# One eighth of a group's output weights as 64-partition rows over the first eight DMA engines

## The chip, the cores and the metric

The kernel runs on one core of one Trainium2 chip. The metric is device time in microseconds (us) of a whole execution. Single executions of one kernel agree within about 0.1% (the six of the kernel before, 382.23 to 382.36), so differences of a few tenths of a microsecond out of 382 need several runs on each side and, better, a look at the trace. Where two times are compared as a ratio, it is the mean time of one kernel's runs over the mean of the other's runs of the same rounds, so it is not quite the ratio of the medians that are quoted.

## The reference, cut to what matters

One token passes through an attention block with a cached K and V and through a gated MLP; a scalar gate mixes the two.

```python
q = (x @ wq)                       # 32 heads of 128
scores = q @ k_cache * Dh ** -0.5  # 4 kv heads, 65536 cached positions
o = softmax(scores) @ v_cache      # 32 x 128 = 4096 numbers
a = o.reshape(1, 1, 4096) @ wo     # wo: 4096 x 1024, bf16, 8 MiB
...
return g * a + (1 - g) * b         # b: the gated MLP
```

K and V caches are 64 MiB each. Almost all the work is to move 162 MB from device memory into SBUF, the on-chip memory.

## The kernel before

A fixed list of large loads is issued by one queue, each as soon as its place in a ring of SBUF is free. The last loads are the four groups of `wo`, the output weights. A group is 1024 rows; partition p holds rows 8p to 8p+7 of it, so column block c (one eighth) of the tile is row 8p+c.

```python
def rows(w, i, c):
    return w[128 * c * i:128 * c * (i + 1), :].rearrange("(p c) n -> p (c n)", c=c)
...
load([("v", 15)], kv(A_v_cache, 15), VB + SUB)
WO_AT = [0, 8 * DO, 16 * DO, 24 * DO]
WO_CUT = [(0, 5), (5, 7), (7, 8)]
for i in range(3):
    load([("wo", i, 0)], rows(A_wo, i, 8), WO_AT[i])
for c0, c1 in WO_CUT:                       # the last group comes in three pieces
    load([("wo", 3, c0)], rows(A_wo, 3, 8)[:, DO * c0:DO * c1], WO_AT[3] + DO * c0)
...
def issue():
    ...
        if n == len(stream) - 1:
            store()                         # an early dummy store of zeros, ahead of the last load
        P("SP", lambda e, ...: e.dma_start(arena[:, o:o + w], src), w=..., dma=...)
...
for i, c0, c1 in [(0, 0, 8), (1, 0, 8), (2, 0, 8)] + [(3, c0, c1) for c0, c1 in WO_CUT]:
    sl, keys = use(("wo", i, c0))
    def f(e, ...):
        for c in range(c0, c1):
            for q in range(4):
                o = DO * (c - c0) + QW * q
                ins = e.matmul(fb[32 * q:32 * q + 1, 0:QW], ovec[:, 8 * i + c:8 * i + c + 1],
                               sl[:, o:o + QW], ...)
        return ins
    P("PE", f, r=[("ovec", i)] + keys, w=["fb"])
P("DVE", lambda e: e.tensor_copy(orow[0:97, :], fb[0:97, 0:QW]), w=["orow", "fb"])
store()
```

## Time and profile before

| | before |
|---|---|
| median of 6 runs (lowest, highest) | 382.30 us (382.23, 382.36) |
| span of the profiled run | 381.1 us |
| last increment of the last weight load | 378.45 us |
| first, mean of the 16 increments of that load | 376.53, 377.44 us |

From the page of the kernel before: the span, the busy time of each engine, and the DMA queues (packets, MB, share of what 16 DMA engines could have been busy). Queue 1 carries the loads; queues 8 and 14 fetch instructions.

```profile
span 381.1 us, 2468 instructions
PE 229.2 (60%) x1383; PEld 55.5 (15%) x793; DVE 204.5 (54%) x162; ACT 22.2 (6%) x23; POOL 7.5 (2%) x35
q1 hardware_dynamic: 4192, 162.01, 98.7%
q8 instruction: 8, 0.13, 0.1%
q14 instruction: 1, 0.01, 0.0%
```

The reader is to see that nothing but the DMA engines is near full, and that the instruction queues look negligible: 0.13 MB out of 162.

Now the end of the run, by stretches of time (busy time of each compute engine, granted PE clock, mean busy share of the 16 DMA engines, GB/s):

```profile
core 0: us, PE busy (x) PEld busy (x) DVE busy (x) ACT busy (x) POOL busy (x), PEclk, DMA share, GB/s
370.00:375.00 5.00, 2.69 (x68) 1.41 (x56) 0.00 (x0) 0.00 (x0) 0.00 (x0) 0.84 0.98 409
375.00:377.00 2.00, 0.26 (x8) 0.22 (x12) 0.00 (x0) 0.00 (x0) 0.00 (x0) 0.50 0.76 305
377.00:378.00 1.00, 1.00 (x24) 0.42 (x20) 0.00 (x0) 0.00 (x0) 0.00 (x0) 0.50 0.34 131
378.00:379.00 1.00, 0.85 (x12) 0.09 (x4) 0.00 (x0) 0.00 (x0) 0.00 (x0) 0.50 0.00 0
```

The share falls in steps, 0.98, 0.76, 0.34: some DMA engines have run out of work while others still load. And the timeline after the last load (start, duration, engine, operation, in brackets what ended the wait):

```profile
378.50 0.09 PEld L718 LDWEIGHTS fbt<-arena 128*1 128x1 bf16 x4 [0.52 <-DMA arena<-in_A_wo_dram]
379.00 0.42 DVE L724 CAST arena<-fbt 97x256 bf16<-97x256 f32 x1 [9.98 <-PE fbt L718]
379.45 0.54 SPq L354 DMA_DIRECT2D out_dram<-arena  x1
```

Four matmuls, a copy and the store follow the last landing at 378.45; this tail takes about 2.6 us to the end of the span. So the time of the kernel is the time of the DMA engine that finishes last, plus 2.6 us.

The trace also has every semaphore increment that a load gives on landing. A full-width load gives 16, and the page counts 16 DMA engines; I read them as one per engine. Those of the last weight load, in us:

```
before  376.53 376.56 376.59 376.61 376.62 376.76 376.90 | 377.63 377.94 377.97 377.99 378.02 378.08 378.12 378.27 378.45
```

Seven engines are early, nine are late, and the gap is about a microsecond. A perfect balance would end at the mean, 377.44, so there is about 1 us to be had, 0.26% of the run.

### The profile page before, as it was taken

The page shows a single profiled execution, that of the slowest core. Times are in us where ns is not written, and L with a number is a line of the kernel's source. Part 1 is how long each engine was busy: PE and PEld are TensorE (multiplying, and loading weights), DVE is VectorE, ACT ScalarE, POOL GpSimd, SP SyncE. Part 2 cuts the span into 40 slices and gives each one's busy share as a digit, 9 for nine tenths or more (in the row PEclk, how much of TensorE's full clock was granted, in tenths as well). Part 3 has the DMA queues.
Part 4 walks back from the last instruction along what each step waited for, and adds up shares of the span by engine and source line. Part 5 has one row for each costly group of instructions (what it writes and reads, how often), then busy time and mean ns, then how long its engine had stood idle before and what let it go on. Part 6 is the DMA issues. An engine that isn't in the chain of part 4 may idle for free.

```text
span 381.1 us, 2468 instructions
## 1 busy us (share of the span) xinstructions
PE 229.2 (60%) x1383; PEld 55.5 (15%) x793; DVE 204.5 (54%) x162; ACT 22.2 (6%) x23; POOL 7.5 (2%) x35
## 2 busy tenths in 40 slices
PE   0050487566558924893887238952995984549373
PEld 0010011111111200121111001220121111212031
DVE  3111596778489525956882249745875871402020
ACT  1000000010420000002000000022000000220000
POOL 4000000000000000000000000000000000000000
PEclk9997599698959975999798858985998896959776
DMA  9999999999999999999999999999999999999995
GB/s 440 434 433 413 426 387 437 440 492 420 428 433 392 426 442 440 433 420 433 454 428 440 440 440 440 421 433 440 392 420 439 457 433 426 426 408 433 423 430 223
DMA packets 4237, 162.15 MB, mean 426 GB/s; under 512 B 508, under 2 KB 516, under 8 KB 772
## 3 DMA queue, kind: packets, MB, share of 16 engines
q1 hardware_dynamic: 4192, 162.01, 98.7%
q8 instruction: 8, 0.13, 0.1%
q10 hardware_dynamic: 36, 0.00, 0.0%
q14 instruction: 1, 0.01, 0.0%
HBM read 162.01 MB, written 0.00 MB: 425 GB/s over the span
## 4 chain that ended last, share of the span: by engine, by line
DMA 63%; DVE 18%; PE 17%; issue 1%; ACTq 0%; SPq 0%; DVEq 0%
DMA arena<-in_A_k_cache_dram 41%; DVE arena L490 15%; DMA arena<-in_A_v_cache_dram 10%; DMA arena<-in_A_wo_dram 8%; PE scp L250 5%; DMA arena<-in_B_b_sp_dram 5%; PE scp L252 5%; PE obt L250 3%; PE obt L252 3%; DVE arena L527 1%; PE fbt L718 1%; ACTq L276 0%; DVE arena L563 0%; DVE arena L561 0%; SPq L377 0%
## 5 line engine op out<-in xcount | busy, mean ns | idle before, releaser
L490 DVE STREAM_TRANSPOSE arena<-arena 128x2048 f32<-128x2048 f32 x64 | 142.8, 2283 | 45.9 <-DMA arena<-in_A_k_cache_dram 31.3
L250 PE MATMUL scp<-arena 128*128 128x512 bf16 x256 | 108.9, 425 | 84.9 <-DVE arena L490 84.9
L252 PE MATMUL scp<-arena 128*128 128x512 bf16 x256 | 107.7, 421 | 0.0
L250 PE MATMUL obt<-arena 128*64 128x512 bf16 (+2 forms) x334 | 62.8, 416 | 21.3 <-DMA arena<-in_A_v_cache_dram 21.3
L252 PE MATMUL obt<-arena 128*64 128x512 bf16 (+2 forms) x334 | 61.9, 410 | 0.0
L250 PEld LDWEIGHTS scp<-arena 128*128 128x128 bf16 x256 | 26.9, 105 | 194.4 <-issue 99.5
L527 DVE STREAM_TRANSPOSE arena<-arena 128x2048 bf16<-128x2048 bf16 x7 | 16.2, 2311 | 31.3 <-PE obt L252 29.1
L250 PEld LDWEIGHTS obt<-arena 128*64 128x64 bf16 (+1 forms) x334 | 18.3, 113 | 74.5 <-issue 56.9
L522 ACT ACTIVATE arena<-arena 128x2048 bf16<-128x2048 f32 x8 | 16.0, 2003 | 218.1 <-DVE arena L519 195.0
L507 DVE TENSOR_SCALAR_CACHE_REDUCE arena<-scp 128x2048 f32<-128x2048 f32 x8 | 18.3, 2292 | 16.0 <-PE scp L252 16.0
L568 PE MATMUL mbt<-arena 128*128 128x128 bf16 x16 | 2.2, 286 | 13.6 <-DVE arena L563 13.6
L530 DVE STREAM_TRANSPOSE arena<-arena 128x1024 bf16<-128x1024 bf16 x2 | 2.5, 1245 | 12.7 <-PE obt L252 12.7
L718 PE MATMUL fbt<-arena 128*1 128x256 bf16 x128 | 6.6, 370 | 4.1 <-DMA arena<-in_A_wo_dram 4.0
L556 DVE RECIPROCAL arena<-mbt 128x1 f32<-128x1 f32 x4 | 0.6, 140 | 15.7 <-PE mbt L551 15.7
L478 POOL COPY arena<-arena 32x32 bf16<-32x32 bf16 x16 | 3.3, 204 | 236.3 <-PE scp L252 210.9
L519 DVE TENSOR_REDUCE arena<-mbt 128x1 f32<-128x32 f32 x4 | 0.8, 192 | 13.3 <-PE mbt L516 13.3
L420 PE MATMUL scp<-arena 8*128 8x1 bf16 x8 | 0.6, 197 | 10.8 <-DVE arena L415 10.8
L425 PE MATMUL mbt<-arena 1*128 1x2 bf16 x1 | 0.2, 158 | 10.4 <-DMA arena<-in_B_b_sp_dram 10.4
L724 DVE CAST arena<-fbt 97x256 bf16<-97x256 f32 x1 | 0.4, 425 | 10.0 <-PE fbt L718 10.0
L427 DVE COPY arena<-mbt 128x2 f32<-128x2 f32 x1 | 0.2, 159 | 10.4 <-PE mbt L425 10.4
L718 PEld LDWEIGHTS fbt<-arena 128*1 128x1 bf16 x128 | 3.3, 103 | 7.2 <-DMA arena<-in_A_wo_dram 3.4
L415 DVE TENSOR_TENSOR arena<-arena 8x1024 bf16<-8x1024 bf16 x1 | 1.2, 1211 | 4.9 <-DMA arena<-in_A_x_dram 4.9
(88 smaller groups left out, 48.9 us busy)
## 6 DMA issues: line engine op xcount, KB each, us to landing
arena<-in_A_k_cache_dram SPq DMA_DIRECT2D x6, 4096.0 KB, 33.2
arena<-in_A_v_cache_dram SPq DMA_DIRECT2D x2, 4096.0 KB, 26.9
arena<-in_B_w_in_dram SPq DMA_DIRECT2D x1, 7168.0 KB, 31.0
arena<-in_A_wo_dram SPq DMA_DIRECT2D x3, 2048.0 KB, 34.4
arena<-in_B_w_out_dram SPq DMA_DIRECT2D x1, 3584.0 KB, 21.8
arena<-in_A_wo_dram SPq DMA_DIRECT2D x1, 1280.0 KB, 31.1
arena<-in_A_wo_dram SPq DMA_DIRECT2D x1, 512.0 KB, 31.8
arena<-in_A_wo_dram SPq DMA_DIRECT2D x1, 256.0 KB, 31.3
```

What stands on the lines that cost most here:

```text
L250: return e.matmul(*a, **kw)
L252: one = e.matmul(*a, **kw).ins
L415: P("DVE", lambda e: e.tensor_tensor(vw(xm, 0, [[128, 8], [1, 128]], 0, 8), vw(xrow, 0, [[0, 8], [1, 128]], 0, 8), vw(idb, 0, [[1, 8], [0, ...
L478: P("POOL", lambda e, pb=pb: e.tensor_copy(vw(qpad, 24 + 32 * pb, [[QP, 4], [1, 8]], 32 * pb, 32), vw(qall, 8 * g, [[32, 4], [1, 8]], 32 * ...
L490: P("DVE", lambda e: e.transpose(ktb(i).bitcast(F32), sl[:, 4096 * p:4096 * (p + 1)].bitcast(F32)), r=keys[4 * p:4 * p + 4], w=[("kt", i % ...
L507: P("DVE", lambda e: e.tensor_scalar(scs(j), scp[:, :], 0.0, None, op0=ALU.add, op1=ALU.max, accum_out=maxc[:, j:j + 1]), w=[("sc", j % 2) ...
L519: P("DVE", lambda e: e.tensor_reduce(gcol(g, K_NB), mb[:, 0:32], AXX, ALU.min), w=[("nb", g), "mb"])
L522: P("ACT", lambda e: e.activation(psb2, scs(j), ACTF.Exp, bias=gcol(j // 2, K_NB), scale=SCALE, accum_out=lp[:, j:j + 1]), r=[("sc", j % 2 ...
L527: P("DVE", lambda e: e.transpose(ptsb2, psb2), r=["psb"], w=[("ptsb", 0), ("ptsb", 1)])
L530: P("DVE", lambda e: e.transpose(ptsb(n), ab("PSB", 1024, 1024 * (n % 2))), r=["psb"], w=[("ptsb", n % 2)])
L568: ins = e.matmul(mb[:, 0:128], sel[:, 128 * c:128 * (c + 1)], osc[:, 128 * c:128 * (c + 1)], start=(c == 0), stop=(c == 3))
L718: ins = e.matmul(fb[32 * q:32 * q + 1, 0:QW], ovec[:, 8 * i + c:8 * i + c + 1], sl[:, o:o + QW], start=False, stop=(i == 3 and c == 7), ti ...
```

## The change

The intent is to let the early engines do some of the work of the late ones. Block c=0 of group 0 (256 KB) leaves the full-width load. It comes back, after the load of group 2, as four loads of 32 rows of 2 KB into partitions 0 to 63, with a source pattern whose outermost dimension is 8, meant to split a load over eight engines. The vector has to be regrouped for it (two small matmuls with a permutation and a copy), and eight matmuls over 64 partitions replace four over 128. The dummy store is halved.

```diff
+    def load_low(key, i, c, off):
+        n = len(stream)
+        place[key] = (n, off, 2 * DO)
+        parts = []
+        for h in range(2):
+            for b in range(2):
+                r0 = 1024 * i + 512 * h + 256 * b
+                src = A_wo[r0:r0 + 256, :].rearrange("(p a c) n -> a p c n", a=8, c=8)[:, :, c, :]
+                o = OFF["RING"] + off + DO * h
+                dst = arena[32 * b:32 * (b + 1), o:o + DO]
+                parts.append((dst, src))
+        stream.append(((key,), off, parts))
...
-    for i in range(3):
+    load([("wo", 0, 1)], rows(A_wo, 0, 8)[:, DO:8 * DO], WO_AT[0] + DO)
+    for i in (1, 2):
         load([("wo", i, 0)], rows(A_wo, i, 8), WO_AT[i])
+    load_low(("wol", 0), 0, 0, 2 * SUB)
...
-                store()
+                store(2)
...
+    def out_down():                     # regroup: ov0[j, h] = the o that belongs to row j of half h
+        def f(e):
+            for h in range(2):
+                ins = e.matmul(mb[0:64, h:h + 1], perm[:, 64 * h:64 * (h + 1)], ovec[:, 0:1], ...)
+            return ins
+        P("PE", f, r=["perm", ("ovec", 0)], w=["mb"])
+        P("DVE", lambda e: e.tensor_copy(ov0[0:64, :], mb[0:64, 0:2]), w=["ov0", "mb"])
...
+    def wo_low():
+        ...
+            for h in range(2):
+                for q in range(4):
+                    o = DO * h + QW * q
+                    ins = e.matmul(fb[32 * q:32 * q + 1, 0:QW], ov0[0:64, h:h + 1], sl[0:64, o:o + QW], ...)
...
-    for i, c0, c1 in [(0, 0, 8), (1, 0, 8), (2, 0, 8)] + ...
+    for i, c0, c1 in [(0, 1, 8), (1, 0, 8), (2, 0, 8)] + ...
+        if (i, c0) == (3, 0):
+            wo_low()
```

(The cuts leave out the bookkeeping for a load in four parts and the permutation that POOL builds at the start.)

More of the change, by code (lines that the diff above doesn't have):

```diff
@@ L28, in __init__, with op @@
         self.ahead = 0
-    def op(self, eng, fn, r=(), w=(), dma=None):
+    def op(self, eng, fn, r=(), w=(), dma=None, parts=1):
         o = Op()
@@ L49, in op @@
         if dma is not None:
-            self.dma_count[dma] = self.dma_count.get(dma, 0) + 16
+            self.dma_count[dma] = self.dma_count.get(dma, 0) + 16 * parts
             o.dma = (dma, self.dma_count[dma])
@@ L111, in run @@
                 if o.dma:
-                    last.then_inc(dsem[o.dma[0]], 16)
+                    for x in last if isinstance(last, list) else [last]:
+                        x.then_inc(dsem[o.dma[0]], 16)
                 elif o.inc:
@@ L188, in bass_gated_mix__gqa_block_cached__mixer_gmlp__decode_kernel @@
         ("MAXC", 2 * total), ("LP", 2 * total), ("COLS", 2 * 64), ("DM", 64), ("ONES", 256), ("QALL", 128), ("OV", OC), ("MHALF", 4),
-        ("YB", FC), ("OROW", QW),
+        ("YB", FC), ("OROW", QW), ("OV0", 2), ("PERM", 128),
     ]:
@@ L212, in bass_gated_mix__gqa_block_cached__mixer_gmlp__decode_kernel @@
     yb, ovec, orow = ab("YB", FC), ab("OV", OC), ab("OROW", QW)
-    dm = af("DM", 32)
+    dm, ov0, perm = af("DM", 32), ab("OV0", 2), ab("PERM", 128)
     psb, psb2 = ab("PSB", 1024), ab("PSB", 2048)
@@ L263, in bass_gated_mix__gqa_block_cached__mixer_gmlp__decode_kernel @@
     P("POOL", lambda e: e.tensor_copy(idb, idf), r=["idf"], w=["idb"])
+    P("POOL", lambda e: e.tensor_copy(vw(perm, 0, [[32, 4], [4, 8], [1, 4]]), vw(idb, 0, [[32, 4], [1, 8], [8, 4]])),
+      r=["idb"], w=["perm"])
     P("POOL", lambda e: e.memset(qpad, 0.0), w=["qpad"])
@@ L345, in bass_gated_mix__gqa_block_cached__mixer_gmlp__decode_kernel, with store @@
     WO_CUT = [(0, 5), (5, 7), (7, 8)]
-    for i in range(3):
+    load([("wo", 0, 1)], rows(A_wo, 0, 8)[:, DO:8 * DO], WO_AT[0] + DO)
+    for i in (1, 2):
         load([("wo", i, 0)], rows(A_wo, i, 8), WO_AT[i])
+    load_low(("wol", 0), 0, 0, 2 * SUB)
     for c0, c1 in WO_CUT:
         load([("wo", 3, c0)], rows(A_wo, 3, 8)[:, DO * c0:DO * c1], WO_AT[3] + DO * c0)
-    osrc = bass.AP(tensor=arena, offset=OFF["OROW"], ap=[[32 * NA, 4], [1, QW]])
-    def store():
-        P("SP", lambda e: e.dma_start(out[0, 0].rearrange("(q n) -> q n", n=QW), osrc), r=["orow"],
+    def store(n):
+        src = bass.AP(tensor=arena, offset=OFF["OROW"], ap=[[32 * NA, n], [1, QW]])
+        P("SP", lambda e: e.dma_start(out[0, 0, 0:n * QW].rearrange("(q n) -> q n", n=QW), src), r=["orow"],
           w=["out"], dma="out")
@@ L368, in issue @@
             keys, off, src = stream[n]
-            w = src.shape[1]
+            w = 2 * DO if isinstance(src, list) else src.shape[1]
             gr = grains(off, w)
@@ L375, in issue @@
             if n == len(stream) - 1:
-                store()
-            P("SP", lambda e, o=OFF["RING"] + off, w=w, src=src: e.dma_start(arena[:, o:o + w], src),
-              w=[("slot", x) for x in gr], dma="s%d" % gr[0])
+                store(2)
+            todo = src if isinstance(src, list) else [(arena[:, OFF["RING"] + off:OFF["RING"] + off + w], src)]
+            P("SP", lambda e, todo=todo: [e.dma_start(dst, x) for dst, x in todo],
+              w=[("slot", x) for x in gr], dma="s%d" % gr[0], parts=len(todo))
             issued[0] += 1
@@ L580, in out_fourth @@
         P("DVE", red, r=["psb"], w=[("ovec", g)])
+    def out_down():
+        def f(e):
+            for h in range(2):
+                ins = e.matmul(mb[0:64, h:h + 1], perm[:, 64 * h:64 * (h + 1)], ovec[:, 0:1],
+                               start=True, stop=True)
+            return ins
+        P("PE", f, r=["perm", ("ovec", 0)], w=["mb"])
+        P("DVE", lambda e: e.tensor_copy(ov0[0:64, :], mb[0:64, 0:2]), w=["ov0", "mb"])
     def mixer_piece():
@@ L702, in bass_gated_mix__gqa_block_cached__mixer_gmlp__decode_kernel @@
     exp_pair(7)
+    out_down()
     for n in (12, 13, 14, 15):
@@ L708, in bass_gated_mix__gqa_block_cached__mixer_gmlp__decode_kernel, with f @@
     out_rest(3)
-    for i, c0, c1 in [(0, 0, 8), (1, 0, 8), (2, 0, 8)] + [(3, c0, c1) for c0, c1 in WO_CUT]:
+    def wo_low():
+        sl, keys = use(("wol", 0))
+        def f(e):
+            for h in range(2):
+                for q in range(4):
+                    o = DO * h + QW * q
+                    ins = e.matmul(fb[32 * q:32 * q + 1, 0:QW], ov0[0:64, h:h + 1], sl[0:64, o:o + QW],
+                                   start=False, stop=False, tile_position=(0, 32 * q), skip_group_check=True)
+            return ins
+        P("PE", f, r=["ov0"] + keys, w=["fb"])
+        done(("wol", 0))
+    for i, c0, c1 in [(0, 1, 8), (1, 0, 8), (2, 0, 8)] + [(3, c0, c1) for c0, c1 in WO_CUT]:
+        if (i, c0) == (3, 0):
+            wo_low()
         sl, keys = use(("wo", i, c0))
@@ L724, in bass_gated_mix__gqa_block_cached__mixer_gmlp__decode_kernel @@
     P("DVE", lambda e: e.tensor_copy(orow[0:97, :], fb[0:97, 0:QW]), w=["orow", "fb"])
-    store()
+    store(4)
     R.ahead = 2
```

## The prediction

> **What bounds the kernel now.** The DMA engines. The page gives them 98.7% of the span on the main queue and 425 GB/s; PE is busy 60%, DVE 54%. Near the end, in the table of windows, DMA is at 0.98 until 375 us, then 0.92, 0.61, 0.34 and 0 in the four microseconds from 375 to 379: the engines do not finish together. In the chain of waits the last weight load is followed by a fixed tail: the timeline has four matmuls at 378.50, the copy of the result at 379.00, the store issued at 379.45, the end at 381.1.
>
> **Which engines are late.** The last weight load's 16 semaphore increments (one per engine) arrive at 376.53 to 376.90 for seven engines, 377.63 for one, 377.94 to 378.45 for eight. My reason is instruction fetches: the packet records show eight of 16 KB on queue 8, each 0.94 to 1.10 us, and the next data packet of that engine is stretched (2624 ns for 2116 at 54.05 us), about 1.45 us lost per fetch. [...] One 8 KB fetch on queue 14 at 87.77 us, then a stretched packet (3080 ns for 2418), costs about 1 us: that fits the single engine at 377.63. The early dummy store uses four engines; its increments come at 376.09, 376.17, 376.30 and 377.19, so three of those four engines are early and the fourth is the one at 377.63. So I read the first eight engines as seven early ones plus that one, and the last eight as the late ones.
>
> **What the change moves.** 256 KB of weights (16 KB per engine) leave a full-width load and come back as four loads of 32 rows of 2 KB. [...] Per engine, estimated from packets of before: 16 KB inside long packets cost 0.60 us (65536 bytes in 2415 ns), a 2 KB packet costs 80 ns. Engines 8 to 15 lose 0.60 us; engines 0 to 7 gain 16 x 80 ns - 0.60 = +0.70 us with semaphore packets.
>
> New last landing: late eight 377.34 to 377.85; early seven 377.2 to 377.6; the single one 377.63 + 0.70 = 378.33. So the last landing goes only from 378.45 to about 378.33: most of the possible 0.6 us is eaten by the one engine of the lower eight that is already late.
>
> **Off the path.** Two matmuls and a small copy to regroup the vector, eight narrow matmuls for four, a POOL copy: all under idle time. The weight loads now wait for one more V piece (about 348.4 instead of 347 us), but loads land some 30 us after issue, so the queue does not run dry.
> **Predicted:** 382.1 us, 8 in 10 within 381.6 to 382.45. Faster by over 2%: 0.003; within 2%: 0.99; slower: 0.007.
>
> **What would show it.** Last load's increments bunched within about 0.7 us with one straggler near 378.3; bytes unchanged; the share of DMA in the last microseconds higher before 377; the tail after the last landing unchanged at about 2.6 us.
>
> **What would make it wrong.** The fetches falling on other engines after the change (more PE instructions), the 8 KB fetch on an upper engine (gain 0.6 us), narrow loads slower than 80 ns per row, or the split not being eight engines.

The last landing is 377.63 + 0.70 = 378.33 us, 0.12 less than 378.45, which from 382.30 gives 382.2; the forecast was 382.1. The split over eight was a premise when this was written; the trace of the changed kernel shows it afterwards (eight increments a load). "Engines 0 to 7" and "8 to 15" name the two groups; no record gives an engine's number. The 80 ns of a 2 KB packet was an estimate: the 128 such packets of the kernel before took 84 to 88 ns.

## The result, and the profile after

| | before | after |
|---|---|---|
| median (lowest, highest) of 6 runs | 382.30 us (382.23, 382.36) | 382.86 us (382.62, 382.99) |
| span of the profiled run | 381.1 us | 381.7 us |
| increments of the last load: first, mean, last | 376.53, 377.44, 378.45 | 375.81, 377.45, 378.99 |

The ratio of after to before is 1.0014 (95% interval 1.0001 to 1.0027): within 2%, but slower, not faster, and outside my range. The same lines of the page, of the changed kernel:

```profile
span 381.7 us, 2486 instructions
PE 231.3 (61%) x1389; PEld 56.0 (15%) x799; DVE 204.7 (54%) x163; ACT 22.2 (6%) x23; POOL 7.9 (2%) x36
q1 hardware_dynamic: 4348, 162.01, 98.6%
q8 instruction: 8, 0.13, 0.1%
q14 instruction: 1, 0.01, 0.0%
```

The same bytes, 156 more packets, the same nine instruction fetches. Its last stretches:

```profile
core 0: us, PE busy (x) PEld busy (x) DVE busy (x) ACT busy (x) POOL busy (x), PEclk, DMA share, GB/s
370.00:375.00 5.00, 3.04 (x76) 1.62 (x68) 0.00 (x0) 0.00 (x0) 0.00 (x0) 0.84 0.97 394
375.00:377.00 2.00, 0.00 (x0) 0.00 (x0) 0.00 (x0) 0.00 (x0) 0.00 (x0) 0.50 0.85 342
377.00:378.00 1.00, 0.72 (x16) 0.54 (x20) 0.00 (x0) 0.00 (x0) 0.00 (x0) 0.50 0.21 82
378.00:379.00 1.00, 0.99 (x20) 0.11 (x10) 0.00 (x0) 0.00 (x0) 0.00 (x0) 0.50 0.04 16
```

Between 375 and 377 the engines are busier than before (0.85 against 0.76), from 377 to 378 less so (0.21 against 0.34), as the change intended. But a new sliver has appeared from 378 to 379: 0.04, where there was 0.00. That is a few engines, working alone, and they decide:

```profile
379.03 0.09 PEld L762 LDWEIGHTS fbt<-arena 128*1 128x1 bf16 x4 [0.53 <-DMA arena<-in_A_wo_dram]
379.54 0.42 DVE L768 CAST arena<-fbt 97x256 bf16<-97x256 f32 x1 [10.28 <-PE fbt L762]
379.99 0.58 SPq L372 DMA_DIRECT2D out_dram<-arena  x1
```

Everything in the tail is 0.53 or 0.54 us later than before, by the same amount as the last landing. The increments of the last load:

```
before  376.53 376.56 376.59 376.61 376.62 376.76 376.90 377.63 377.94 377.97 377.99 378.02 378.08 378.12 378.27 378.45
after   375.81 376.04 377.11 377.20 377.27 377.29 377.30 377.34 377.48 377.51 377.57 377.63 377.84 378.24 378.66 378.99
```

The mean has not moved (377.44 and 377.45), the spread has grown. There are two engines that finish very early and three stragglers, at 378.24, 378.66 and 378.99. I had expected one straggler, at 378.33.

**Following the engines.** The trace's packet records do not name their engine, but most packets start 3 or 4 ns before the recorded end of another, and I take the two to be of one engine. So they can be strung into 16 chains. By "the first eight" I mean the eight engines that carry a load that is split over eight; the records don't give their numbers. The engines of the dummy stores of two, four and eight rows I take to be among them. Two things mark them: the two loads of eight rows at the start of the kernel (eight increments each), and, in the changed kernel, sixteen more packets of 2 KB per chain at the end. In the changed kernel the eight chains with 2 KB packets to spare are the eight that carry the marks of the start. (Some chains come within a nanosecond of each other and can be swapped there, so in the full kernels I trust the group of a chain at the end and not each fetch's ordinal.) Followed backwards from the end, where 2 KB packets tell the groups, all three stragglers belong to the first eight; its other five land from 377.11 to 377.30, and the last eight are the two very early ones and the six from 377.34 to 377.84. The chains that end last, with the increments 378.66 and 378.99, are thus of the first eight, and each of them holds a 16 KB instruction fetch, by my stringing those at 135.9 and 194.4 us. So the group that got more work was not free of PE fetches. (I call the 16 KB fetches on queue 8 PE's, because leaving out PE instructions leaves two of the eight, as the last experiment shows.) That is theory A: an engine ends when its own list ends, an engine that carried an instruction fetch is about 1.4 us late (in the kernel before the fetch at 53.13 us took 0.94 us, and a data packet after it, at 54.05, 2624 ns where those beside it took 2116), and two of the first eight had carried one. Theory B is that narrow loads are costly in themselves (four instructions instead of none, issued later, small rows). Theory C is that the added small work lengthens the tail. The experiments start from there.

That fetches make engines late can be counted in the kernel before alone. At each load, count the increments that come more than 0.85 us after the first one:

```
kernel before: fetches at  53.1 | 87.8 (8 KB), 99.9 | 136.3 | 191.8 | 247.3 | 287.2 | 337.4 | 371.8
load landing at            57.7 | 105.0             | 143.7 | 201.8 | 259.9 | 289.0 | 337.4 | 374.6
late engines               1    | 3                 | 4     | 5     | 6     | 7     | 8     | 9
```

The landing is the first increment of a load; the fetch at 337.4 us shows in that load's last increment, at 339.55. At the load of 40.7 us there is none. Every fetch makes one more late engine, and none of them catches up, because each engine's list has no slack (the DMA share is 0.97 or more in every stretch up to 375 us).

### The profile page after: what moved, and what is told of

Same layout as the page of the kernel before. It is cut to its first block, busy times and chain, and to the rows that moved or that the text cites. A ratio compares the mean times of both kernels' runs of the same rounds, so it can differ in the third digit from the quotient of the medians.

```text
span 381.7 us, 2486 instructions
## 1 busy us (share of the span) xinstructions
PE 231.3 (61%) x1389; PEld 56.0 (15%) x799; DVE 204.7 (54%) x163; ACT 22.2 (6%) x23; POOL 7.9 (2%) x36
## 3 DMA queue, kind: packets, MB, share of 16 engines
q1 hardware_dynamic: 4348, 162.01, 98.6%
## 4 chain that ended last, share of the span: by engine, by line
DMA 62%; PE 18%; DVE 18%; SPq 1%; issue 1%; ACTq 0%; DVEq 0%
DMA arena<-in_A_k_cache_dram 41%; DVE arena L509 15%; DMA arena<-in_A_v_cache_dram 9%; DMA arena<-in_A_wo_dram 7%; PE scp L251 5%; DMA arena<-in_B_b_sp_dram 5%; PE scp L253 5%; PE obt L251 4%; PE obt L253 4%; DVE arena L546 1%; SPq L396 1%; PE fbt L762 1%; ACTq L279 0%; DVE arena L580 0%; DVE arena L582 0%
## 5 line engine op out<-in xcount | busy, mean ns | idle before, releaser
L251 PE MATMUL obt<-arena 128*64 128x512 bf16 (+2 forms) x334 | 63.5, 420 | 19.5 <-DMA arena<-in_A_v_cache_dram 19.5
L253 PE MATMUL obt<-arena 128*64 128x512 bf16 (+2 forms) x334 | 62.8, 416 | 0.0
```

Of the source, the lines that this page charges most:

```text
L251: return e.matmul(*a, **kw)
L253: one = e.matmul(*a, **kw).ins
```

## The experiments

Eleven kernels were run, in three lots with the kernel before beside each (medians 382.42, 382.30 and 382.43 us in the three). All results but those of the two kernels that leave out matmuls on purpose were correct.

### The changed kernel again

No edit.

> The changed kernel once more, to see whether the engines that carry the instruction fetches are the same in a second profile. Theory A (each engine runs through its own list; an engine that carried an instruction fetch is about 1.45 us late, and the change gave 0.7 us more work to engines of the first eight that were already late): time 382.6 to 383.0, and the last landing near 379.0 belongs to an engine of the first eight that carried a fetch. If fetches sit on other engines this time, the last landing moves with them. Theory B (the narrow loads themselves are slow: more DMA instructions, issued later, small rows) and theory C (the added matmuls and copies lengthen the tail): 382.6 to 383.0 wherever the fetches are.

Measured: 382.88 us (382.77 to 382.92), ratio to before 1.0012 (0.9998 to 1.0026). The last increments are 378.37, 378.83 and 378.83. By the chains, the increments again have five of the first eight between 377.3 and 377.6, then three stragglers of the first eight; of the last eight two are very early (375.96 and 376.42) and six lie between 377.58 and 377.87. So the result repeats, and with the same make-up: of the first eight engines three are late, of the last eight six.

### The same loads over 16 engines

```diff
-    ...rearrange("(p a c) n -> a p c n", a=8, c=8)[:, :, c, :]
+    ...rearrange("(p a c) n -> a p c n", a=16, c=8)[:, :, c, :]
```

(with the permutation that belongs to it)

> The same four narrow loads of 32 rows of 2 KB, the same matmuls, the same wait, but each load is split over 16 engines instead of 8, so every engine moves the bytes it moved before. Theory A: the time returns to that of the kernel before within 0.15 us, 382.2 to 382.45 (eight 2 KB packets cost 80 ns instead of 75 ns of a long packet, so +0.04 us), last landing near 378.5. Theories B and C: nothing is gained, 382.8 to 382.9.

Measured: 384.23 us (383.70 to 384.35), ratio 1.0046 (1.0033 to 1.0058); last increment 380.25. Neither theory said so: A expected 382.2 to 382.45, B and C 382.8 to 382.9. This kernel takes the imbalance away and loses 1.8 us. The stretches of time of this run show how:

```profile
core 0: us, PE busy (x) PEld busy (x) DVE busy (x) ACT busy (x) POOL busy (x), PEclk, DMA share, GB/s
370.00:375.00 5.00, 1.82 (x48) 1.06 (x40) 0.00 (x0) 0.00 (x0) 0.00 (x0) 0.84 1.00 282
375.00:377.00 2.00, 1.68 (x32) 0.52 (x24) 0.00 (x0) 0.00 (x0) 0.00 (x0) 0.50 0.95 394
```

The engines are fully busy from 370 to 375 us (1.00) but move 282 GB/s, where the changed kernel moved 394 at 0.97. In the packet records, 85 of the 256 packets of 2 KB took more than 95 ns, up to 271, where in the changed kernel all lie between 84 and 93. The 10 KB packets beside them have a median of 426 ns (a tenth of them 676 or more) instead of 388. So this was no clean control: splitting 32 partitions over 16 engines (queue 1 has 4380 packets instead of 4348, eight more increments a load) brought something new. Theory D: it depends on the partitions whether an engine's packets are slow. As I read the pattern, a load over eight engines gives each engine four neighbouring partitions, one over sixteen gives it two. The mechanism is not shown by any trace; that the partitions decide at all is a theory here, and the run with the upper partitions, below, tests it.

### Half of the loads over 16 engines

```diff
-    ..., a=8, c=8)
+    ..., a=(8, 16)[h], c=8)
```

> Two of the four narrow loads stay on 8 engines, two go over 16: the first eight engines get +0.36 us instead of +0.70 against before, the last eight -0.28 instead of -0.60. Theory A, with the fetches where the changed kernel's trace has them: last landing 378.99 - 0.34 = 378.65, time about 382.5. Theories B and C: 382.8 to 382.9 (the number of loads, rows and matmuls is unchanged).

Measured: 383.61 us (383.50 to 383.74), ratio 1.0032 (1.0019 to 1.0044); last increment 379.61 instead of the 378.65 expected. It holds two of the loads of the last experiment and shows the same: 2 KB packets up to 227 ns, 10 KB packets with a median of 413.5 ns. As a test of A against B it is void.

### Over the first four and the first two engines

```diff
-        for h in range(2):
-            for b in range(2):
-                ...
+        for p0, np_, a in ((0, 40, 4), (40, 24, 2), (64, 64, 16)):
+            src = A_wo[1024 * i + 8 * p0:...].rearrange("(p a c) n -> a p c n", a=a, c=8)[:, :, c, :]
+            dst = arena[p0 % 64:p0 % 64 + np_, o:o + DO]
```

> The eighth as three loads: 64 rows over 16 engines, 40 rows over the first four, 24 rows over the first two, which carried no PE fetch in either trace (the store over two engines landed early). Against before: engines 4 to 15 -0.28 us, engines 2 and 3 +0.5, engines 0 and 1 +1.5. Theory A: every engine ends at or below 377.94, last landing 378.2 to 378.4, time 382.0 to 382.2, faster than both kernels, unless a PE fetch falls on engines 0 to 3 in this build (then 382.8 to 383.5). Theories B and C: 382.7 or more.

Measured: 383.57 us (383.41 to 383.75), ratio 1.0031 (1.0018 to 1.0043); last increment 379.42. A miss with slow packets again: 2 KB packets took up to 204 ns. (By the pattern, one engine's share of the two narrow loads is ten or twelve neighbouring partitions; which engine wrote them is not shown.)

### The eighth as a full-width load of its own

```diff
-    load_low(("wol", 0), 0, 0, 2 * SUB)
+    load([("wol", 0)], rows(A_wo, 0, 8)[:, 0:DO], 2 * SUB)
...
+            for q in range(4):     # in wo_low, 128 partitions
+                ins = e.matmul(fb[...], ovec[:, 0:1], sl[:, QW * q:QW * (q + 1)], ...)
```

The regrouping stays, though its result is not used.

> The spread over 16 engines slowed packets (2 KB packets of up to 178 ns beside 84), so it changed more than the bytes per engine. Here the eighth is one load of its own over all 128 partitions, at the place and with the wait of the narrow loads, 2 KB rows, eight per engine; the regrouping matmuls and the small copy stay. Theory A (each engine's own sum; the slowest decides): all 2 KB packets near 84 ns, last landing 378.4 to 378.6, time 382.3 to 382.5, as before. Theory C (the added small work and the later wait cost the time): 382.8. [...]

Measured: 382.42 us (382.36 to 382.62), ratio 1.0003 (0.9989 to 1.0017); last increment 378.66 in the profiled run, which was the slowest of the five. The packets of 2 KB all lie between 84 and 92 ns. (The longest 2 KB packet of the spread kernel is the 271 ns given above, not the 178 of this expectation.) The load is 128 rows of 2 KB, eight for each of 16 engines, as the four loads of the spread kernel are together, from the same place in the queue:

```profile
core 0: us, PE busy (x) PEld busy (x) DVE busy (x) ACT busy (x) POOL busy (x), PEclk, DMA share, GB/s
370.00:375.00 5.00, 2.62 (x72) 1.55 (x60) 0.00 (x0) 0.00 (x0) 0.00 (x0) 0.90 0.98 402
```

402 GB/s, not 282. This is the control that the spread kernel should have been. With the balance restored, 0.44 us of the 0.56 that the change cost are gone (382.86 to 382.42), though the wait for the later V piece, the small matmuls, the copy and the 2 KB rows are all still there. That leaves theory C about 0.1 us. By itself it does not separate A from B, since the narrow loads went too; the next three do.

### Marking the first eight engines in the kernel before

```diff
-                store()
+                mark()        # the dummy store with 8 rows of 256 bytes instead of 4 of 512
```

> The kernel before, but the early dummy store has 8 rows of 256 bytes instead of 4 of 512, so it runs on the first eight engines and its increments show when each of them gets there. My prediction read seven early and one late among the first eight. Theory A as it stands after the changed kernel's trace: five early (near 376.1 to 376.3), one near 377.2 (the 8 KB fetch), two at 377.5 or later (with a PE fetch). Time 382.3 as before.

Measured: 382.32 us (382.20 to 382.40), ratio 1.0001 (0.9988 to 1.0013), so the mark costs nothing. The store of eight rows gives eight increments, which I take to be those of the first eight engines. Its increments, and those of the last load that follows on every engine:

```
mark, first eight   376.07 376.13 376.16 376.21 376.24 377.46 377.66 377.93
last load, all      376.54 376.58 376.59 376.59 376.68 376.69 376.69 377.90 378.01 378.08 378.09 378.11 378.16 378.19 378.33 378.36
```

Five of the first eight are early and three are late. The last load follows the mark on its engine after 0.43 to 0.47 us (376.07 to 376.54 for the first), so the engine at 377.93 should be the one at 378.36: in this run the very last engine is one of the first eight (if it is the one at 378.33, the last but one). My prediction's map, seven early and one late, is wrong here without the change, so no move of the fetches is needed to explain the result. In the profile that the prediction used, the groups of the nine late engines were not read, and which one is last can differ from this one.

### Two eighths over the first eight engines

```diff
+    load_low(("wol", 1), 0, 1, 2 * SUB + 2 * DO)
-    load([("wo", 0, 1)], rows(A_wo, 0, 8)[:, DO:8 * DO], WO_AT[0] + DO)
+    load([("wo", 0, 2)], rows(A_wo, 0, 8)[:, 2 * DO:8 * DO], WO_AT[0] + 2 * DO)
```

> Two eighths instead of one go over the first eight engines alone. Theory A: those engines get another 0.70 us, so last landing 378.99 + 0.70 = 379.7 and time 383.5 to 383.7; all 2 KB packets stay near 84 ns. Theory B (it is the number of narrow loads, not the balance): each four cost 0.5, so 383.3 to 383.4. A rival in which the late engines are in the last eight (my prediction's premise): 383.0.

Measured: 383.65 us (383.51 to 383.95), ratio 1.0037 (1.0024 to 1.0049); increments of the last load:

```
double  375.27 375.87 376.64 376.77 376.95 377.02 377.07 377.27 377.93 378.05 378.14 378.19 378.36 379.44 379.63 379.63
```

The last landing is 379.63, where A said 379.7; the packets of 2 KB stay between 84 and 95 ns. By the ends of the chains, the eight earliest values are now those of the last eight engines, fetches and all; then come five of the first eight (377.93 to 378.36), and then, alone, the three late ones. Theory B's number, 383.3 to 383.4, lies just below the runs, and the premise of my prediction (late engines among the last eight) would have given 383.0.

### A version for the first four engines

```diff
+        for s in range(8):
+            src = A_wo[..., 0:QW].rearrange("(p a c) n -> a p c n", a=4, c=8)[:, :, c, :]
+            parts.append((arena[0:16, o:o + QW], src))
```

Only 64 KB move (256 columns of the eighth), as eight loads of 16 rows of 512 bytes, by the pattern four rows for each of four engines.

> A version that follows theory A: 64 KB (the first 256 columns of the eighth) as eight loads of 16 rows of 512 bytes over the first four engines alone, which carried no PE fetch[...]. The others lose 0.15 us, engines 0 to 3 gain about 0.65[...]. Theory A: last landing 378.45 - 0.15 = 378.30 (engine of the 8 KB fetch at 378.3), time 382.1 to 382.3, not slower than before and below the changed kernel. Theory B (narrow loads cost in themselves): 383 or more, with eight of them.

Measured: 382.37 us (382.24 to 382.70), ratio 1.0004 (0.9991 to 1.0016). In the profiled run, which was the fastest, the last landing was 378.22 and the time 382.24, as A said; but the other four runs took 382.29 to 382.70, and there is no gain over before in the median. As a faster version it is inconclusive at best. It does speak against theory B: eight narrow loads, twice as many as in the change, cost nothing that can be seen. (The 0.65 us of the expectation was an estimate whose ground is a time for a 512-byte packet given without its source; the eight such packets of the kernel before, in stores, took 27 to 34 ns. The 378.3 for the engine of the 8 KB fetch, 377.63 + 0.65, would rest on it too.)

### The narrow loads into the upper partitions

```diff
-                dst = arena[32 * b:32 * (b + 1), o:o + DO]
+                dst = arena[64 + 32 * b:64 + 32 * (b + 1), o:o + DO]
```

> The change with one thing different: the four narrow loads still run on the first eight engines, same rows and bytes, but land in partitions 64 to 127[...]. Theory D[...]: 2 KB packets and the packets beside them well above 84 ns and 388 ns, time above the change, 383.0 to 383.8. If only the number of engines and the bytes matter: 2 KB packets near 84 ns, 382.8 to 382.9.

Measured: 385.15 us (384.95 to 385.20), ratio 1.0070 (1.0057 to 1.0082); last increment 380.96. Same rows, same bytes, same source pattern and as many packets on queue 1 (4348), other partitions, and 2.3 us more than the change (385.15 against 382.86). 106 of the 256 packets of 2 KB took more than 110 ns, most of those 150 to 182, about twice the usual 84, and the 10 KB packets have a median of 523.5 ns instead of 388.

```profile
core 0: us, PE busy (x) PEld busy (x) DVE busy (x) ACT busy (x) POOL busy (x), PEclk, DMA share, GB/s
370.00:375.00 5.00, 1.70 (x41) 1.00 (x36) 0.00 (x0) 0.00 (x0) 0.00 (x0) 0.84 1.03 249
```

Busy share 1.03 and 249 GB/s: the time that the packets lose is recorded as busy time. Theory D said that it would be slower, though less (383.0 to 383.8). With that pattern the rows are fast into partitions 0 to 63 (2 KB packets of 84 to 93 ns in the changed kernel) and slow into 64 to 127, this run shows; why is not shown. The change had avoided it with partitions 0 to 63.

### Both kernels with most matmuls left out

```diff
-            for fe in range(4):        # K pieces: 3 or 2 instructions instead of 12
+            for fe in range(1):
-            for i in range(16):        # V pieces
+            for i in (0, 15):
-            for c in range(c0, c1):    # wo
+            for c in range(c0, c1 if c1 - c0 <= 2 else c0 + 1):
```

(and one of two halves of each V block, and two of eight blocks for the query and MLP input weights). The results are wrong; every load is kept. It takes away what is suspected: with few PE instructions there should be little to fetch.

> Wrong results on purpose: the kernel before with most of its matmuls left out (about 450 PE instructions instead of 2176), all loads kept. Theory A: instead of eight 16 KB fetches there are one or two, and the last load's increments show that many late engines (plus the one of the 8 KB fetch): 13 or 14 near 376.6 to 377.0, the rest 377.6 to 378.5. Because one late engine is enough to hold the end, the time falls little: 381.9 to 382.3. If the late engines had another cause than the fetches, eight or nine would still be late.

> Wrong results on purpose: the changed kernel with the same matmuls left out. Theory A: the first eight engines end 0.7 us later than in the cut kernel before and the last eight 0.6 us earlier, each; last landing 379.0 if the fetch falls on the first eight (382.8), 378.3 or less if it falls on the last eight (382.1 or less). The bulk of each group shows the +0.7 and -0.6 without any fetch in between: the first eight near 377.3 to 377.6, the last eight near 376.0 to 376.3.

Measured: 382.26 us (382.12 to 382.36) for the cut kernel before, ratio to before 0.9995 (0.9982 to 1.0009), and 382.33 us (382.32 to 382.75) for the cut changed kernel, ratio to before 1.0002 (0.9989 to 1.0014). The page of the cut kernel before, and then that of the cut changed kernel, on the instruction queues:

```profile
q8 instruction: 2, 0.03, 0.0%
q14 instruction: 1, 0.01, 0.0%
```

```profile
q8 instruction: 2, 0.03, 0.0%
q14 instruction: 1, 0.01, 0.0%
```

Two 16 KB fetches instead of eight, and the one of 8 KB. The increments of the last load:

```
cut before  376.52 376.54 376.59 376.60 376.64 376.66 376.67 376.70 376.75 376.77 376.79 376.88 376.89 | 377.73 378.02 378.31
cut after   375.90 375.95 376.01 376.16 376.31 376.36 | 377.13 377.13 377.15 377.29 377.34 377.47 377.48 377.49 377.72 378.34
```

Three fetches, three late engines, thirteen early ones within 0.37 us of each other: the fetches are the cause of the lateness. In the cut kernel before, 377.73 is the engine of the 8 KB fetch, in the first eight (its mark of the dummy store is at 377.30). By my stringing both PE fetches fell on the last eight there, but this is not shown: apart from the store's four marks all chains carry the same bytes at the end, and at 53.19 us packets of two chains, one of each group, begin in the same nanosecond, on the way to the fetch at 97.4 us.

In the cut changed kernel the bytes tell the groups: the six early values and the two with a PE fetch (377.48 or 377.49, and 377.72) are the last eight; 377.13 to 377.49 are seven of the first eight; 378.34 is the engine of the 8 KB fetch. So here, where the first eight are what my prediction took them to be, the last landing is 378.34, and the prediction said 378.33. (An agreement within 0.01 us is partly luck: the engine came from 377.73, not 377.63, and gained 0.61 us, not 0.70.)

The time of the cut changed kernel is that of the cut kernel before within 0.07 us, with the same narrow loads and small work as in the change, which speaks against theories B and C once more. But its five runs fall in two sets, 382.32 to 382.33 and 382.71 and 382.75, and only one of the first set was profiled. The expectation had 382.8 for a fetch on the first eight: the two longer runs would fit that, and then the engine of a fetch changes from run to run, but no trace shows it. (For a fetch on the last eight it had 382.1 or less, which is 0.2 us too low.)

In both cut kernels the time barely falls although PE's busy time falls from 229 to 77 us (231 to 78 in the changed one) and six of the nine fetches are gone, because one late engine is enough to hold the end.

## Why the prediction was right or wrong

- **What bounds the kernel: right.** The DMA engines, and of these the one that ends last, plus a fixed tail. From before to after the last landing moved by 0.54 us (378.45 to 378.99), and the median time by 0.56.
- **Where lateness comes from: right.** Each instruction fetch makes one more late engine (the count above, from 1 after the fetch at 53.1 us to 9 after the last), and with two PE fetches instead of eight there are three late engines instead of nine.
- **How the load is split: right.** Eight engines got sixteen more packets of 2 KB each, by the chains, and the four loads gave 32 increments.
- **What each engine gains and loses: right.** I had +0.70 and -0.60 us. Between the two cut kernels, by the ends of the chains, the seven engines of the first eight without a fetch ended 0.69 us later on average (376.13 to 376.82), the six of the last eight without a fetch 0.66 earlier (376.30 to 375.64), and the engine of the 8 KB fetch 0.60 later. (The groups of the cut kernel before are not certain. Against the mean of all its thirteen engines without a fetch, 376.21, it is 0.61 later and 0.57 earlier.) Doubling the change added 0.64 us to the last landing (378.99 to 379.63).
- **Which engines are late: wrong, and this is the step that failed.** The prediction said: "So I read the first eight engines as seven early ones plus that one, and the last eight as the late ones." The reading came from a store that uses only four engines (four increments). It showed three early and one late, and I filled in the other four to suit the numbers, because eight early or nearly early engines and eight late ones looked like the two halves. In its place the runs show five early and three late among the first eight: in the mark's run without the change, and in the changed kernel itself, with 378.24, 378.66 and 378.99. So the last landing was not the 8 KB engine's 378.33 but that of an engine with a PE fetch, at 378.99. Less the 0.69 us that the first eight gained, the two with a PE fetch would have ended near 378.0 and 378.3.
- **Off the path: right within 0.1 us.** With a balanced load in place of the narrow ones, the later wait and the small work left 0.12 us against before (382.42 and 382.30). The wait ended about when I said (issues from 348.78 us), but the last load was issued only at 353.40 instead of 347.15, because six issues, four of them the narrow loads, come between. It still landed 25.6 us later, so the queue did not run dry.
- **What would make it wrong.** I had named fetches falling on other engines after the change. Nothing shows that they moved: the mark's run has the same count without the change, so the map was wrong from the start. Four marks say nothing of the other four engines of the half.

What stays open: how the engine of a fetch is chosen. The full kernels whose groups can be told at the end (the marked one, the change twice, the doubled change) all have three late engines in the first eight, the cut changed kernel one, and no run shows the rule. Nor is it shown which engine was last in the very profile that the prediction read.

## What to carry to other kernels

In this kernel, bound by its loads, the time was set by the one DMA engine that ended last (last landing 0.54 us later, median time 0.56), and 0.13 MB of instruction fetches made the difference between early and late engines. Where a kernel is like this one, look at the 16 landing increments of the last load, not at the mean share. Before work is moved from one set of engines to another, mark the sets in a run and read which engines are late; do not fill the map in by symmetry. And look at the packet times when a load is narrowed or goes to other partitions: with the narrow loads in partitions 64 to 127 the slow ones of the 2 KB packets took mostly 150 to 182 ns instead of 84, and the run 2.3 us more than the change, while balance could have gained about 1 us.
